# Own float32 tiles for the first six feature tiles' weights in a fused Mamba-2 and SwiGLU kernel, with a new order of steps

## The chip, the cores and the metric

The kernel runs on one NeuronCore of a Trainium2 chip. The metric is the device time of one execution in microseconds, lower is better. The engines named below are PE (TensorE matmuls; PEld its weight loads), DVE (VectorE), ACT (ScalarE), POOL (GpSimd) and SP (the queue from which nearly all DMAs are issued). Each engine works through its own queue in program order, and waits for the others by semaphores.

## What is computed

Two stages with a reshape between them. The first is a chunked state-space scan for 4 batches, 8 heads, 768 tokens, head dimension 32 and state dimension 16. The second is a SwiGLU feed-forward of 3072 tokens, width 256 and 1536 features.

```python
# stage 1, per chunk of tokens (x, a, B, C)
cum = np.cumsum(np.log(a_chunk), axis=-1)
L = np.exp(cum[..., :, None] - cum[..., None, :]) * causal
y = ((Cc @ Bc.T) * L) @ xc + (Cc @ state) * np.exp(cum)
state = np.exp(sum_la) * state + (Bc * np.exp(cum_last - cum)).T @ xc
# stage 2, x = y as (3072, 256)
xn = x / np.sqrt(mean(x * x) + 1e-6) * rms_g
out = (silu(xn @ w_gate) * (xn @ w_val)) @ w_out
```

The three weight matrices of stage 2 are double precision in memory, so they arrive as pairs of 32-bit words, and the kernel makes float32 values of them on the chip.

## The kernel before, in words

The 3072 tokens are six blocks of 512, and the 1536 features twelve tiles of 128 (`f` from 0 to 11), in six pairs (`j`). The program is a list of 1451 short steps, written out as one string, `order`; a loop at the end calls the function behind each step, and this order is the order of every engine's queue. A step is `block:name.numbers`, with `/slot` for one of three double banks of PSUM. The string was written for this program as a whole, so nothing reorders it later.

**Decoding weights.** There are 20 pieces: 0 to 3 are gate and value columns 0 to 127 and 128 to 255, 4 to 13 are the five further 256-column groups (even numbers gate, odd ones value), 14 to 19 are `w_out`. For each piece, `fetch` loads the words by a DMA on SP, `pow` (three ACT instructions) makes the exponents, `man` (two DVE instructions) the mantissas, and `wt` (one DVE instruction) their product. For gate and value columns below 768, `keep` then copies the float32 result by a DMA on SP into the big tile `wgv`, which is declared as fp32r. In the kernel before, `wt` writes columns 0 to 255 into the tile `wearly`, and columns 256 to 767 over the mantissa tile `m`, of which there are two buffers. `wearly` has the tag `sw3`: it shares its memory with the split weights of pair 3.

**Feature tiles 0 to 5 of block 0** are full float32 products (lines 868 and 878) that read `wgv` after the `keep`: `early.f.s` for tiles 0 and 1, on tokens not yet normalised (`norm.f` on DVE scales them afterwards), and `gate.f` for tiles 2 to 5. `silu.f` (ACT) and `hid.f` (DVE) finish each.

**All other feature products** use operands split in a leading and a trailing part. `sw.j.k` (three DVE instructions) splits a weight, and `kt.j.k` (a DMA) writes its leading part to `wgv`. `xm`, `xs`, `xh`, `xl` split the tokens. `D.f.k` (line 952) is the cross product, `W.f.k` (ACT, line 956) scales it, `G.f.k` (line 963) adds the main products, then come `silu` or `silug` and `hid` or `hidg`. They begin once `switch.0` and `switch.1` have given up the first two slots of PSUM, that is after `hid.5`.

**Stage 1** works on pairs of chunks: `bc` and `x` load B, C and x; `turn`, `T`, `Tt` transpose; `mask`, `sums`, `exp` make decays; `g`, `gg` the C-B products and `L`, `L1` their decay on DVE; `scale`, `A`, `S` the states; `y.p` the outputs. For later pairs decays make a round trip through DRAM: `row`, `rowe`, `rowout` store them, `dT` and `spread` load them, `Td` uses `dT`. At the start, `a` is loaded, turned (`aT`), clipped (`la0`) and its logarithm taken; from it come `c`/`cx`, `d`/`dx` and `r`/`parts`.

**From one block to the next**: after the last `y`, `sq`, `ms`, `rs` take the norm, `rb` spreads it by a round trip through DRAM, `xn` applies it, and the splits follow; meanwhile PE works on the output products `o` (block 0, line 975) or `O` (line 1033) of the running block.

**DMA semaphores.** SP and the four loads issued by ACT (half of `bc.0` and `bc.1`) share eight semaphores in turn. Each DMA instruction first waits until the DMA before it on its semaphore has landed, so at most eight are under way, and all that stands behind a waiting one on its queue waits too.

Of the kernel before, what the change touches and what calls it, by code (L numbers as in the profile page):

```python
# [21 lines left out]
def kernel(  # L22
# [33 lines left out]
    nc = tc.nc  # L56
# [79 lines left out]
    wg, wv = wgvf[:, 0], wgvf[:, 1]  # L136
    wearly = const.tile([P, 2, 2, 256], FP32, tag="sw3", name="wearly")
# [15 lines left out]
    def fetch(*ks):  # L153
        for k in ks:
            n, c, w = pieces[k]
            if n == "o":
                src, dst, shape = wsrc[n][:, c:c + w], wo[:, c:c + w], (w, DM)
            else:
                src = wsrc[n][:, :, 2 * c:2 * (c + w)]
                dst = wearly[:, "gv".index(n), :, c:c + w] if c < 256 else None  # L160
                shape = (2, w)
# [49 lines left out]
    def keep(k):  # L211
        n, c, w = pieces[k]
        src = wearly[:, "gv".index(n), :, c:c + w] if c < 256 else parts.pop((k, "w"))
        nc.sync.dma_start(out=wgv[:, "gv".index(n), :, c:c + w].bitcast(FP32), in_=src)
# [648 lines left out]
    def products_gv(f, gv):  # L863
        ps["gv", f] = gv
        fs = slice(f * P, (f + 1) * P)
        for k, w in enumerate((wg, wv)):
            for t in range(2):
                nc.tensor.matmul(out=gv[:, k], lhsT=w[:, t, fs], rhs=xns[0][:, t],  # L868
                                 start=(t == 0), stop=(t == 1))


    def products_early(f, s, gv):
        ps["gv", f] = gv
        fs = slice(f * P, (f + 1) * P)
        tk = slice(s * 256, s * 256 + 256)
        for k, w in enumerate((wg, wv)):
            for t in range(2):
                nc.tensor.matmul(out=gv[:, k, tk], lhsT=w[:, t, fs], rhs=yts[0][:, t, tk],
# [320 lines left out]
    def of_chunk(n, fn):  # L1199
# [40 lines left out]
        0:sq.1 0:pow.6 0:man.3 0:wt.2 0:pow.3 0:mask.3/1 0:early.0.0/0 0:keep.2 0:yt.1 0:bc.2  # L1240
        0:mask.2/2 0:parts.1 0:sums.3 0:man.6 0:wt.6 0:exp.3 0:wt.3 0:ms.0 0:fetch.13 0:early.0.1
        0:keep.6 0:keep.3 0:row.0 0:rowe.1 0:rowout.1 0:turn.2 0:sums.2 0:fetch.9 0:rs.0 0:T.2
        0:man.4 0:scale.2 0:early.1.0/1 0:wt.4 0:keep.4 0:norm.0 0:xn.0 0:exp.2 0:xm.0.0 0:ydone.1
        0:early.1.1 0:Tt.2.0 0:fetch.8 0:pow.7 0:xs.0.0 0:x.2 0:man.7 0:silu.0 0:rowe.0 0:fetch.10
        0:wt.7 0:gate.2/0 0:keep.7 0:pow.9 0:rowout.0 0:man.9 0:wt.9 0:sw.3.1 0:dT.2 0:hid.0
        0:Tt.2.1 0:norm.1 0:pow.8 0:bc.4 0:xm.0.1 0:man.8 0:wt.8 0:sw.3.0 0:gate.3/2 0:man.10
        0:silu.1 0:Td.2 0:xs.0.1 0:hid.1 0:pow.10 0:wt.10 0:gg.2/1 0:silu.2 0:L1.2.2 0:fetch.11
        0:kt.3.1 0:L1.2.3 0:xh.0.0 0:xh.0.1 0:hid.2 0:kt.3.0 0:A.2 0:pow.11 0:silu.3 0:pow.12
        0:scale.4 0:L.2.0 0:sw.4.0 0:man.11 0:fetch.14 0:wt.11 0:gate.4/1 0:hid.3 0:silu.4 0:man.12
        0:hid.4 0:x.3 0:S.2 0:bc.3 0:ydone.0 0:gate.5/0 0:silu.5 0:scale.3 0:y.2/2 0:xl.0.0 0:hid.5  # L1250
        0:yt.2 0:sq.2 0:ydone.2 0:switch.1 0:switch.0 0:D.6.0 0:dT.3 0:D.6.1 0:bc.5 0:W.6.0 0:D.7.0
# [151 lines left out]
```

## Time and profile before

| | us |
|---|---|
| three runs, median | 433.31 |
| three runs, lowest and highest | 427.08 and 433.46 |
| the profiled execution, as timed | 433.31 |
| its span, first to last instruction | 431.6 |

The execution's time is 1.7 us above its span. Some points in that span, from the timeline of each engine:

| point | us from the start |
|---|---|
| `la0`, the clipped logarithm's input | 4.4 to 4.8 |
| `d`, first products from the logarithms | 12.2 to 13.5 |
| `y.0` begins on PE | 32.7 |
| `gate.2` begins | 53.1 |
| second half of `gg.2` begins | 69.0 |
| `gate.5` ends | 82.5 |
| `hid.5` ends; first `D` of block 0 | 83.9; 84.2 |
| `y.3` ends | 94.2 |
| `o.11` ends | 134.5 |
| first `D` of blocks 1 to 5 | 123.1, 188.0, 253.8, 314.5, 372.6 |

"PEclk" in the views is the share of full clock that was granted to TensorE. Where it is 0.50, a matmul takes about twice as long. The busy time of PE is modelled from pipelined instructions and can hide that.

### The profile page before, as it was taken

To read this page: it belongs to the slowest core of one execution; us is meant where nothing else is said; L and a number is where in the kernel's file an instruction comes from. 1 tells how busy PE (TensorE), PEld (TensorE's weight loads), DVE (VectorE), ACT (ScalarE), POOL (GpSimd) and SP (SyncE) were. 2 spreads that over 40 slices of the span, in tenths; PEclk is the share of its full clock that TensorE was granted. 3 is DMA by queue.
4 is the path that set the end of the run, shared out by engine and by line. 5 is a ranking of instruction groups with operands and counts; after the bars stand their busy time and mean duration, and the time that the engine had idled before them with its cause. 6 is when DMAs were issued, how large, how long until landed. Compare 5 with 4: busy or idle time off the path is not lost.

```text
span 431.6 us, 9229 instructions
## 1 busy us (share of the span) xinstructions
PE 400.3 (93%) x3749; PEld 318.5 (74%) x3749; DVE 255.9 (59%) x545; ACT 256.9 (60%) x450; POOL 38.4 (9%) x57
## 2 busy tenths in 40 slices
PE   6797964999899999899979999998999989999997
PEld 3465722578688788897758997877987869978897
DVE  5555869799899547864355863446823434713551
ACT  1766787297998648265548644666674536366310
POOL 2201000010032001120011210100130001000000
PEclk9657895899999999999999999999999999999999
DMA  8725869659427228300154100203000001100001
GB/s 146 191 55 137 245 128 205 108 167 222 123 80 121 50 49 148 57 14 0 27 125 87 31 24 10 79 2 115 2 26 0 2 2 31 51 24 2 0 2 49
DMA packets 98034, 31.69 MB, mean 73 GB/s; under 512 B 77608, under 2 KB 91816, under 8 KB 97992
## 3 DMA queue, kind: packets, MB, share of 16 engines
q1 hardware_dynamic: 93832, 30.85, 30.6%
q10 hardware_dynamic: 4160, 0.26, 0.7%
q8 instruction: 29, 0.48, 0.5%
q14 instruction: 13, 0.11, 0.1%
HBM read 22.64 MB, written 3.74 MB: 61 GB/s over the span
## 4 chain that ended last, share of the span: by engine, by line
PE 72%; DVE 10%; ACT 7%; DMA 3%; issue 3%; SPq 3%; ACTq 0%; DVEq 0%
PE gv L963 24%; PE o L1033 18%; PE gv L952 13%; PE o L975 3%; PE y L711 3%; PE gate L868 2%; SPq L122 1%; PE g L567 1%; PE g L574 1%; DVE m L200 1%; DMA wr<-in_moe_w_val_dram 1%; DVE S L663 1%; DMA roots<-r 1%; DVE L L479 1%; DMA cr<-in_C_dram 1%
## 5 line engine op out<-in xcount | busy, mean ns | idle before, releaser
L963 PE MATMUL gv<-xh,wgv 128*128 128x512 f32 x264 | 109.1, 413 | 3.4 <-DMA wgv<-top 2.0
L963 PE MATMUL gv<-xl,mw 128*128 128x512 f32 x264 | 104.5, 396 | 0.0
L956 ACT ACTIVATE gv<-gv 128x512 f32<-128x512 f32 x132 | 73.7, 587 | 40.6 <-PE gv L952 40.0
L971 DVE SCALAR_TENSOR_TENSOR h<-gv,u 128x512 f32<-128x512 f32 x66 | 45.2, 689 | 81.3 <-PE gv L963 72.4
L952 PE MATMUL gv<-xs,sw 128*128 128x512 f32 x264 | 79.0, 411 | 2.8 <-DVE h L971 2.5
L968 ACT ACTIVATE u<-gv 128x512 f32<-128x512 f32 x66 | 39.5, 603 | 45.8 <-PE gv L963 43.9
L963 PEld LDWEIGHTS gv<-xh,wgv 128*128 128x128 f32 x264 | 50.1, 190 | 20.0 <-ACT gv L956 9.4
L952 PEld LDWEIGHTS gv<-xs,sw 128*128 128x128 f32 x264 | 45.9, 189 | 15.5 <-DVE h L971 4.0
L963 PEld LDWEIGHTS gv<-xl,mw 128*128 128x128 f32 x264 | 50.2, 190 | 9.4 <-DVE xl L848 0.2
L487 POOL TENSOR_SCALAR_AFFINE_SELECT L<-L 64x512 f32<-64x512 f32 x32 | 24.4, 762 | 115.3 <-ACT L L485 113.8
L1033 PE MATMUL o<-two,s 128*128 128x128 f32 x240 | 32.7, 277 | 1.3 <-DVE s L999 0.8
L1033 PE MATMUL o<-wo,h 128*128 128x128 f32 x240 | 33.8, 275 | 0.0
L1033 PEld LDWEIGHTS o<-two,s 128*128 128x128 f32 x240 | 30.1, 191 | 3.1 <-DVE s L999 1.2
L1033 PEld LDWEIGHTS o<-wo,h 128*128 128x128 f32 x240 | 31.2, 191 | 1.6 <-ACT u L968 0.4
L1033 PE MATMUL o<-two,h 128*128 128x128 f32 x240 | 30.8, 276 | 0.1
L1033 PEld LDWEIGHTS o<-two,h 128*128 128x128 f32 x240 | 28.8, 192 | 0.6 <-DVE h L1003 0.2
L1049 ACT COPY v<-o 128x256 f32<-128x256 f32 x15 | 5.6, 372 | 37.0 <-PE o L1033 37.0
L761 POOL TENSOR_TENSOR sq<-sq,sq 128x512 f32<-128x512 f32 (+1 forms) x6 | 7.4, 1236 | 169.9 <-issue 88.1
L975 PE MATMUL o<-wo,h 128*128 128x256 f32 x96 | 22.2, 379 | 0.0
L975 PEld LDWEIGHTS o<-wo,h 128*128 128x128 f32 x96 | 18.2, 189 | 2.8
L1006 DVE TENSOR_TENSOR s<-s,h 128x256 f32<-128x256 f32 x30 | 14.7, 518 | 8.9 <-PE o L1033 8.9
L1060 DVE TENSOR_TENSOR ob<-v,o 128x256 f32<-128x256 f32 x18 | 7.3, 416 | 18.5 <-PE o L1033 17.5
(183 smaller groups left out, 567.2 us busy)
## 6 DMA issues: line engine op xcount, KB each, us to landing
L<-rowd SPq DMA_DIRECT2D x32, 128.0 KB, 3.8
xr<-in_x_dram SPq DMA_DIRECT2D x24, 128.0 KB, 4.3
wgv<-top SPq DMA_DIRECT2D x12, 256.0 KB, 4.1
wr<-in_moe_w_out_dram SPq DMA_DIRECT2D x6, 512.0 KB
wr<-in_moe_w_val_dram SPq DMA_DIRECT2D x5, 512.0 KB
wr<-in_moe_w_gate_dram SPq DMA_DIRECT2D x5, 512.0 KB, 5.8
out_dram<-ob SPq DMA_DIRECT2D x9, 256.0 KB, 2.2
br<-in_B_dram SPq DMA_DIRECT2D x22, 64.0 KB, 3.4
```

The costliest lines, as they stand in the source:

```text
L487: nc.gpsimd.affine_select(out=L[r], in_=L[r], pattern=[[0, NH], [1, HC]], compare_op=ALU.is_ge, fill=0.0, base=0, channel_multiplier=-1)
L711: nc.tensor.matmul(out=y[2 * k + u][rows, (2 * n + i) * HC:(2 * n + i + 1) * HC], start=(k, u, rows.start) not in opened, stop=True, skip_ ...
L761: nc.gpsimd.tensor_tensor(out=sqs[blk][:, tk], in0=sqs[blk][:, tk], in1=sq2, op=ALU.add)
L868: nc.tensor.matmul(out=gv[:, k], lhsT=w[:, t, fs], rhs=xns[0][:, t], start=(t == 0), stop=(t == 1))
L952: nc.tensor.matmul(out=g, lhsT=Sw[f // 2][:, k, t, (f % 2) * P:(f % 2 + 1) * P], rhs=xs[blk][:, t], start=(t == 0), stop=True, skip_group_ ...
L956: nc.scalar.activation(out=GV[f, k], in_=GV[f, k], func=AF.Copy, scale=-BETA * BETA / (BETA + 1.0))
L963: nc.tensor.matmul(out=GV[f, k], lhsT=lhsT, rhs=rhs, start=False, stop=True, skip_group_check=True)
L968: nc.scalar.activation(out=us[f], in_=GV.pop((f, 0)), func=AF.Silu, scale=ONE)
L971: nc.vector.scalar_tensor_tensor(out=hidden_of(blk, f), in0=GV.pop((f, 1)), scalar=ONE, in1=us.pop(f), op0=ALU.mult, op1=ALU.mult)
L975: nc.tensor.matmul(out=o, lhsT=hs_[blk, f // 2][:, f % 2, k // 2, (k % 2) * P:(k % 2 + 1) * P], rhs=wo[:, f], start=opens, stop=(f == NF - ...
L1006: nc.vector.tensor_tensor(out=Sh[j], in0=Sh[j], in1=tiles_of_h(blk, j)[0], op=ALU.subtract)
L1033: nc.tensor.matmul(out=o[t] if apart else o[:, t * P:(t + 1) * P], lhsT=lhsT[:, t], rhs=rhs, start=(k in (1, 2, 4, 5) and j == 0 and (apar ...
```

## The change

The float32 weights of columns 0 to 767 get three tiles of their own, `whole_w[0..2]`, of 256 columns each. They carry the tags `sw3`, `sw4` and `sw5`, and so share memory with the split weights of pairs 3, 4 and 5; before, only `wearly` did so, with pair 3. `wt` writes there, the float32 products read there, and `keep` copies from there to `wgv`.

```diff
-    wg, wv = wgvf[:, 0], wgvf[:, 1]
-    wearly = const.tile([P, 2, 2, 256], FP32, tag="sw3", name="wearly")
+    whole_w = [const.tile([P, 2, 2, 256], FP32, tag="sw%d" % (j + NF // 4), name="whole_w")
+               for j in range(NF // 4)]
+
+    def whole(n, c, w):
+        return whole_w[c // 256][:, "gv".index(n), :, c % 256:c % 256 + w]
...
-                dst = wearly[:, "gv".index(n), :, c:c + w] if c < 256 else None
+                dst = whole(n, c, w) if c < DF // 2 else None
...
     def keep(k):
         n, c, w = pieces[k]
-        src = wearly[:, "gv".index(n), :, c:c + w] if c < 256 else parts.pop((k, "w"))
-        nc.sync.dma_start(out=wgv[:, "gv".index(n), :, c:c + w].bitcast(FP32), in_=src)
+        nc.sync.dma_start(out=wgvf[:, "gv".index(n), :, c:c + w], in_=whole(n, c, w))
...
-        for k, w in enumerate((wg, wv)):
+        for k, n in enumerate("gv"):
             for t in range(2):
-                nc.tensor.matmul(out=gv[:, k], lhsT=w[:, t, fs], rhs=xns[0][:, t],
+                nc.tensor.matmul(out=gv[:, k], lhsT=whole(n, f * P, P)[:, t], rhs=xns[0][:, t],
                                  start=(t == 0), stop=(t == 1))
...
-                nc.tensor.matmul(out=gv[:, k, tk], lhsT=w[:, t, fs], rhs=yts[0][:, t, tk],
+                nc.tensor.matmul(out=gv[:, k, tk], lhsT=whole(n, f * P, P)[:, t], rhs=yts[0][:, t, tk],
```

All lines of `order` are new: it holds the same 1451 steps in another order (slots apart). The stretch up to the end of `y.3` in both:

```diff
-        0:warm 0:zeros 0:a 0:never 0:idle.7 0:ones 0:ident 0:after 0:whole16 0:kinks 2:exps
-        0:ident16 0:hmask 0:fetch.5 0:whole 0:mask.0.0/0 0:eps 0:upto 0:mid 0:upto2 0:bc.0 0:tmask
-        0:fetch.0 0:aT 0:la0 0:x.1 0:mask.1.1/2 0:log 0:log4.0.4 0:head 0:mask.0.1/1 0:log4.4.2
-        0:c*2 0:after2 0:mids 0:r.0 0:d 0:bc.1 0:turn.0.1 0:part 0:x.0 0:cx 0:part2 0:man.5 0:sel
...
-        0:sq.1 0:pow.6 0:man.3 0:wt.2 0:pow.3 0:mask.3/1 0:early.0.0/0 0:keep.2 0:yt.1 0:bc.2
-        0:mask.2/2 0:parts.1 0:sums.3 0:man.6 0:wt.6 0:exp.3 0:wt.3 0:ms.0 0:fetch.13 0:early.0.1
-        0:keep.6 0:keep.3 0:row.0 0:rowe.1 0:rowout.1 0:turn.2 0:sums.2 0:fetch.9 0:rs.0 0:T.2
-        0:man.4 0:scale.2 0:early.1.0/1 0:wt.4 0:keep.4 0:norm.0 0:xn.0 0:exp.2 0:xm.0.0 0:ydone.1
-        0:early.1.1 0:Tt.2.0 0:fetch.8 0:pow.7 0:xs.0.0 0:x.2 0:man.7 0:silu.0 0:rowe.0 0:fetch.10
-        0:wt.7 0:gate.2/0 0:keep.7 0:pow.9 0:rowout.0 0:man.9 0:wt.9 0:sw.3.1 0:dT.2 0:hid.0
-        0:Tt.2.1 0:norm.1 0:pow.8 0:bc.4 0:xm.0.1 0:man.8 0:wt.8 0:sw.3.0 0:gate.3/2 0:man.10
-        0:silu.1 0:Td.2 0:xs.0.1 0:hid.1 0:pow.10 0:wt.10 0:gg.2/1 0:silu.2 0:L1.2.2 0:fetch.11
...
+        0:warm 0:a 0:set 0:bc.0 0:ident 0:bc.1 0:ones 0:x.0 0:zeros 0:mean 0:head 0:upto 0:x.1
+        0:never 0:after 0:mid 0:fetch.0 0:upto2 0:mids 0:ident16 0:idle.7 0:fetch.1 0:whole16
+        0:mask.0.0/0 0:whole 0:hmask 0:tmask 0:part 0:gcol 0:part2 0:sel 0:mask.1.1/2 0:after2 0:aT
+        0:kinks 0:la0 0:mask.0.1/1 0:log4.0.4 0:fetch.5 0:r.0 0:eps 0:parts.0 0:log 0:d 0:log4.4.2
+        0:dx 0:c*2 0:cx 0:scale.0 0:log4.6.2 0:turn.0.1 0:bc.2 0:T.0.1 0:Tt.0.0.1 0:sums.0.1
...
+        0:r.1 0:y.0/1 0:yt.0 0:keep.5 0:sq.0 0:y.1/2 0:rowe.0 0:fetch.4 0:pow.6 0:dT.2 0:wt.1
+        0:keep.1 0:parts.1 0:mask.3/1 0:sums.3 0:sq.1 0:early.0.0/0 0:man.2 0:yt.1 0:pow.2 0:scale.2
+        0:rowout.0 0:pow.9 0:man.6 0:wt.6 0:ms.0 0:wt.2 0:keep.2 0:early.0.1 0:man.3 0:man.9 0:exp.3
+        0:wt.9 0:rs.0 0:norm.0 0:pow.3 0:wt.3 0:fetch.8 0:bc.3 0:turn.2 0:xn.0 0:xm.0.0 0:pow.4
+        0:man.4 0:mask.2/2 0:sums.2 0:exp.2 0:wt.4 0:keep.3 0:early.1.0/1 0:early.1.1 0:xs.0.0
+        0:norm.1 0:x.2 0:fetch.10 0:T.2 0:Tt.2.0 0:silu.0 0:hid.0 0:pow.7 0:man.7 0:wt.7 0:Tt.2.1
+        0:xh.0.0 0:Td.2 0:gate.2/0 0:xm.0.1 0:gg.2/1 0:keep.7 0:silu.2 0:pow.8 0:gate.3/2 0:sw.3.1
+        0:hid.2 0:fetch.12 0:kt.3.1 0:man.8 0:wt.8 0:x.3 0:L1.2.2 0:keep.6 0:L1.2.3 0:L.2.0 0:A.2
+        0:gate.4/1 0:sw.3.0 0:xh.0.1 0:fetch.11 0:silu.1 0:hid.1 0:S.2 0:gate.5/0 0:keep.4 0:silu.3
+        0:fetch.13 0:scale.3 0:y.2/2 3:table 0:xs.0.1 0:pow.10 0:man.10 0:wt.10 0:silu.4 0:man.11
+        0:pow.11 0:hid.3 0:silu.5 0:pow.12 0:sq.2 0:ydone.2 0:kt.3.0 0:hid.4 0:xl.0.0 0:xl.0.1
+        0:ydone.0 0:hid.5 0:ydone.1 0:switch.1 0:switch.0 0:D.7.0 0:D.6.0 0:W.6.0 0:sw.4.0 0:wt.11
+        0:sw.4.1 0:W.7.0 0:yt.2 0:x.4 0:man.12 0:wt.12 0:D.6.1 0:fetch.14 0:G.6.0 0:bc.5 0:turn.3
+        0:T.3 0:kt.4.0 0:D.7.1 0:Tt.3.0 0:tok 0:D.9.0 0:scale.5 0:silug.6 0:tokout 0:G.7.0 0:W.6.1
+        0:dT.3 0:kt.4.1 0:G.6.1 0:Tt.3.1 0:sw.5.0 0:bc.4 0:kt.5.0 0:Td.3 0:W.7.1 0:S.3 0:silug.7
+        0:x.5 0:W.9.0 0:D.8.0 0:hidg.6 0:G.7.1 0:pow.13 0:fetch.16 0:W.8.0 0:man.13 0:gg.3/2
+        0:L1.3.3 0:D.8.1 0:W.8.1 0:hidg.7 0:G.9.0 0:silug.9 0:pow.14 0:G.8.0 0:silug.8 0:D.10.0
+        0:L.3.0 0:W.10.0 0:L1.3.2 0:scale.4 0:G.8.1 0:y.3/2 0:wt.13 0:sw.5.1 0:fetch.15 0:D.11.0
...
```

Instruction counts in the two programs: PE, DVE, POOL and SP have the same instructions (by kind and shape); ACT has 31 loads of its function tables in place of 36. The numbers of PE, DVE, ACT and DMA instructions per step are otherwise equal. The steps `exps`, `table` and `set` load a table by name; further loads are put in by the compiler where the next ACT function needs another table.

## Prediction

> **What bounds the kernel now.** I read the page's busy shares first, then the windows by stage, then the waits up to the first `D`, then the chain of waits, and last the timelines of single engines.
>
> ```profile
> PE 400.3 (93%) x3749; PEld 318.5 (74%) x3749; DVE 255.9 (59%) x545; ACT 256.9 (60%) x450; POOL 38.4 (9%) x57
> ```
>
> PE is busy 93% of the span, but that is an average over stages. The windows (columns: us, PE, PEld, DVE, ACT, POOL busy, granted clock, DMA share, GB/s):
>
> ```profile
> 0.00:13.00 13.00, 7.45 (x33) 4.38 (x33) 6.29 (x30) 3.30 (x7) 2.94 (x13) 1.00 0.90 147
> 13.00:36.90 23.90, 23.01 (x204) 13.71 (x207) 15.14 (x37) 14.68 (x28) 2.21 (x5) 0.50 0.47 145
> 36.90:64.20 27.30, 21.22 (x167) 12.81 (x158) 18.89 (x37) 23.13 (x34) 1.46 (x2) 0.94 0.66 157
> 64.20:77.80 13.60, 6.75 (x50) 3.33 (x51) 13.12 (x25) 8.50 (x13) 0.00 (x0) 0.50 0.95 183
> 77.80:84.20 6.40, 6.40 (x140) 3.32 (x138) 4.20 (x11) 1.19 (x2) 0.00 (x0) 1.00 0.68 137
> 84.20:134.00 49.80, 47.71 (x383) 38.07 (x382) 46.61 (x92) 44.46 (x79) 6.23 (x6) 1.00 0.57 142
> 164.30:431.60 267.30, 257.50 (x2356) 219.26 (x2354) 134.43 (x283) 141.84 (x250) 21.30 (x27) 0.99 0.15 35
> ```
>
> The late phase is PE's. Between 64.2 and 77.8 the bound is DVE (13.12 of 13.60), with PE half idle at half clock. Between 84.2 and 134 DVE (46.61 of 49.80) and PE (47.71) are both nearly full. The waits up to 84.2 (us in total, times, longest) name the holes:
>
> ```profile
> ACT early L415 <- DMA cr<-in_C_dram: 6.1, 1, 6.1
> PE g L574 <- DVE T L548: 5.1, 1, 5.1
> PE d_ps L391 <- ACT early L415: 4.4, 1, 4.4
> PE g L574 <- DVE h L892: 3.3, 1, 3.3
> ```
>
> The first and third are one hole: ACT must issue half of `bc.1` before it may run `cx`, its issue waits for an earlier load on the same semaphore, and PE's `d` waits for `cx`. The second is `Td.2`. The chain of waits (start, us, what) shows this start, and table loads of ACT in the middle:
>
> ```profile
> 8.03 3.10 DMA cr<-in_C_dram
> 11.16 0.46 ACTq L122
> 11.66 0.53 ACT early L415
> 12.23 0.94 PE d_ps L391 x4
> ...
> 38.41 1.28 ACT L1225
> ...
> 53.19 1.28 ACT L899
> ...
> 55.12 1.28 ACT L1121
> ```
>
> PE's timeline gives the price of half clock: the same sixteen float32 products, `gate.2` and `gate.3`, then `gate.4` and `gate.5`:
>
> ```profile
> 53.05 7.03 PE L868 MATMUL gate<-xn,wgv 128*128 128x512 f32 x16
> 72.97 9.54 PE L868 MATMUL gate<-xn,wgv 128*128 128x512 f32 x16 [1.06 <-DVE L L613]
> ```
>
> **The tiles.** Reading `whole_w` instead of `wgv` removes the wait of each float32 product for the `keep` DMA. It is worth 0: `keep.4` landed at 52.75, `gate.2` began at 53.05 behind PE's own `early.1.1`; `keep.7` landed at 62.2, `gate.4` began at 72.97, released by DVE. If a cover went, a `keep` (issue to landing some 4 us) would be its price. The `keep` stays, for the split products. Added: `sw.4` and `sw.5` now wait until `keep.4` to `keep.7` and `gate.2` to `gate.5` have read the shared memory. Behind a waiting `sw.4.0` on DVE stand `wt.11`, `sw.4.1` and the rest of pair 3; but the order puts `sw.4.0` behind `switch.0`, where `gate.5` and the keeps are past. Direct cost 0; indirect, below.
>
> **The start.** In after, `bc.0` and `bc.1` are issued first and wait only for the load of `a`; ACT need not stall behind `x.1`. Ahead of `la0` DVE has 4.1 us of rows, so `la0` at 6.0 to 6.4 against 4.4, and `d` at about 7.8 against 12.23: −4.4. But steps that lay in the hole now follow: `c*2` (1.25 us, pieces) and `row.0` (1.15, `r_ps` rows) fall into the stretch from `d` to `y.0`, 20.45 us long, where PE is busy 23.01 of 23.90. −4.4 + 2.4 = −2 at `y.0`; bounds −4.4 and 0. Weights come later: eight B and C loads go ahead of `fetch.0`, but `wt.0` is needed by `early.0.0` alone, at 45 us. On SP `fetch.4` moves behind `rowe.0`, which waits for ACT's table and `e_sb` (about 37 us, before 15.9); a weight load of its kind lands 5.8 us after issue (page, part 6), so at 43, and `man.4`, which needs it, ran at 45.3: cost 0, and 2 to 3 us of DVE's wait if `rowe.0` comes late.
>
> **From `y.0` (32.7) to the first `D` (84.2), 51.5 us.** Three terms:
> - *Tables.* Before has four loads here (38.41, 53.19, 55.12, 61.89), after two (at `silu.0`, and `3:table`): 2 × 1.28 = −2.6, since three of the four are on the chain.
> - *`Td.2`.* From the end of `xn.0` (50.62) to `Td.2` (68.50), DVE has 14.4 us of rows. In after `sw.3.1` (1.81), `man.8` (1.11), `wt.8` (0.69), `sw.3.0` (1.81) and `man.10` (1.11), 6.5 us, stand behind it, and some smaller steps: 7.2 us remain. The 5.1 us wait goes. SP issues `dT.2` earlier too.
> - *Clock.* Without that hole `gate.4` and `gate.5` may run at full clock: 9.54 − 7.03 = −2.5.
>
> Sum −10.2. What is late next is DVE itself: its rows from `y.0` to `hid.5` sum to 40.4 before and 37.9 after, at a busy/sum ratio near 0.95. So after cannot be shorter than 37.9 × 0.95 + some 3 us until DVE's first step, 39; that allows −12.5. ACT's rows are 31 and 34, no bound. A new order has waits of its own that no row shows; before lost 51.5 − 39 = 12 to such waits. I take −8 of the 10.2 (bounds −12 and −3): first `D` at about 84.2 − 2 − 8 = 74.
>
> **What the shared memory pushes behind the first `D`.** Before had `sw.4.0` at 72.8, in the lead; in after `sw.4.0`, `sw.4.1`, `sw.5.0` follow `hid.5`. DVE's rows from there to `scale.4`, the last input of `y.3`, sum to 14.9 us after; before, the same stretch (to `L1.3.2`) 9.75, and took 8.1. PE's own rows to the end of `y.3` are 13.1 against 8.6. To the end of `o.11`: DVE 55.8 against 50.4, PE 47.8 against 46.7, taken 49.7. To `1:D.11.1`, PE is the larger: 83.4 against 75.3 (taken 80.1), DVE 76.2 against 67.6. PE's sum over the whole rest is the same in both, 321.3 us (taken 347.4), so the DVE-bound stretch costs only what PE idles: between 14.9 − 13.1 = 1.8 and 55.8 × 0.95 − 47.8 = 5.2. I take +3; bounds 0 and +5.2.
>
> **The late phase.** At each block's end PE lives on products that don't need the next block's norm. Their rows between the last `y` and the next first `D` sum to 27.4, 27.4, 32.4, 38.0 and 16.5 us before (the norm's way took 28.9, 28.5, 37.3, 39.3, 16.6), after to 19.4, 25.1, 38.2, 33.4, 26.1. The shortest cover, 19.4, is above the shortest way that before shows, 16.6. So 0, bounds −4 and +4: the whole late loss of PE is 267.3 − 257.5 = 9.8, and a new order could win or lose some 40% of that. Five table loads fewer in all (36 to 31), three of them before the first `D`; the two late ones, 2.6 us of ACT, cost nothing where PE is the bound.
>
> **Sum.** −2 − 8 + 3 + 0 = −7. The profiled execution ran 433.31 with a span of 431.6, and is itself the median: 433.3 − 7 = 426.3. Bounds of the terms, not all at one end: 419 to 432.
>
> **A rule of the skill.** The trace first: the clock fell at 12.99, after PE idled 4.4 us, and stayed at 0.50 to 36.9 although PE was busy 23.01 of 23.90. The Trainium skill, "TensorE: Matmul & The Clock Gate", Part 1, says otherwise of such a stretch: one window of about 3.4 us with sustained activity releases the throttle, one idle window brings it back. By that rule the clock should have returned by about 20, and a lead without the 4.4 us hole would run at full clock: the sum would be some 10 us lower, by my estimate from this page. The rows say that this lead's small products, spaced by waits on DVE and ACT, do not count as sustained, so I leave the half clock of the lead in the main sum.
>
> **The rivals.**
> 1. *The lead runs at full clock.* Without the hole at 7.8 to 12.2 the gate may never close. For it: full clock from 6.16 to 12.99 with PE busy 7.45 of 13.00. Against: the shares above. From `d` to `y.0` the chain's PE pieces sum to 16 us; at full clock half of that, 8, and one more from the `y` pieces (2.55): 426 − 9 = 417.
> 2. *The gain is hidden.* DVE's rows to `1:D.11.1` are 8.6 us more after; if block 1's first half is held by them, all of the 10 comes back: 433.
> 3. *Slower.* After the switch DVE is the bound and PE idles in pieces, so that the clock halves. It decides where PE idles over about 2 us of a 3.41 us window: between 40.30 and 43.71 PE was busy 1.36, and the next window ran at 0.50. Price: DVE stretch 55.8 and further waits, 8 us where I put 3, and five windows at half clock, 1.7 to 3.4 us each, 8 to 17: −10 + 8 + 13 = +11, 442 to 446. For it: 46.61 of 49.80 already. Against: full clock through that whole window in before.
>
> That the change doesn't do what it says is so in part: the DMA wait that the tiles remove was not one. Whatever comes, comes from the order.
>
> **How the numbers follow.** Main case 0.45, rival 1 0.15, rival 2 0.20, rival 3 0.20. A measurement of this kernel can tell about 2% (its three runs spread by 1.5%): under 424.6, over 442.0. Faster: two fifths of the main case (0.18), rival 1 (0.15) and a little of rival 2: 0.36. Slower: nearly all of rival 3 and a little late loss: 0.20. Same: 0.44. Range 417 to 442: it leaves out half of rival 1 and most of rival 3.
>
> **What would show it.** In the profile after: `d` near 7.8 and no wait of `cx` on a C load; `y.0` near 31; the wait of `g` L574 on `T` L548 gone; two table loads between `y.0` and the first `D`; first `D` near 74; `y.3` 12 to 15 us behind it (before 10); `o.11` 52 to 53 behind it (before 50.3); `wgv` no longer among the products' releasers at L868. The main case's own range is 419 to 432. I am wrong if the first `D` is past 80, if PEclk is 0.50 behind it, or if first `D`s of blocks 2 to 5 drift from each other by more than 4 us against before.

## The result, and the profile after

| | before | after |
|---|---|---|
| median (lowest to highest) of the first comparison, us | 433.38 (427.08 to 438.85) | 407.62 (406.40 to 408.99) |
| profiled execution, us; its span | 433.31; 431.6 | 407.84; 406.1 |
| `d` begins | 12.23 | 6.18 |
| `y.0` begins | 32.68 | 21.91 |
| first `D` of block 0 | 84.18 | 61.73 |
| `o.11` ends | 134.45 | 114.50 |

The ratio of the times is 0.9452, with a 95% interval of 0.9346 to 0.9558; the medians differ by 25.8 us, where 7 were forecast. The ratios, here and below, leave out runs more than 1.5% above the fastest of their kernel, so they differ a little from the quotients of the medians. By stage of the two spans: up to `y.0` −10.8, from there to the first `D` −11.7, from there to the end of `o.11` +2.5, from there on −5.5.

The busy shares of the page, after, with its row of granted clocks (40 equal slices of the span):

```profile
PE 387.1 (95%) x3749; PEld 309.1 (76%) x3749; DVE 252.7 (62%) x545; ACT 248.8 (61%) x445; POOL 36.2 (9%) x57
PEclk9989999999999999999999999999999999999999
```

PE is busy 13 us less with as many products, at a higher clock: in the trace before, 44.4 us of the span are at 0.50, after 3.4. The windows of the four stages (columns as in the prediction), first after, then two of the same stages before:

```profile
0.00:21.90 21.90, 19.08 (x165) 11.22 (x165) 16.75 (x59) 13.83 (x29) 5.08 (x17) 0.98 1.04 166
21.90:61.70 39.80, 33.44 (x419) 19.38 (x418) 36.55 (x74) 31.12 (x50) 1.46 (x2) 0.97 0.81 210
61.70:114.50 52.80, 49.62 (x387) 38.81 (x388) 49.69 (x99) 40.02 (x77) 1.60 (x2) 1.00 0.62 157
114.50:406.10 291.60, 284.98 (x2781) 239.73 (x2779) 149.68 (x315) 163.84 (x292) 28.09 (x36) 1.00 0.17 39
```

```profile
32.70:84.20 51.50, 38.57 (x424) 22.77 (x423) 38.50 (x78) 33.43 (x50) 1.46 (x2) 0.79 0.74 169
134.50:431.60 297.10, 287.30 (x2784) 242.47 (x2782) 151.24 (x316) 161.15 (x290) 25.57 (x32) 0.99 0.17 39
```

In the middle DVE was busy 38.50 us of 51.50 before and 36.55 of 39.80 after. Its idle time fell from 13.0 to 3.25 us (−9.75), and 1.95 us of its work went elsewhere: together the −11.7. In the late stage, from the end of `o.11` on, PE's idle time fell from 9.8 to 6.6.

PE's timeline after, at the places shown of before:

```profile
45.18 0.65 PE L577 MATMUL g<-T 32*64 32x128 f32 x20 [0.23 <-DVE T L551]
45.77 3.70 PE L870 MATMUL gate<-xn,whole_w 128*128 128x512 f32 x8
51.02 7.13 PE L870 MATMUL gate<-xn,whole_w 128*128 128x512 f32 x16 [0.25 <-DVE L L616]
```

The wait for `Td.2` is 0.23 us where it was 5.07, and `gate.4` with `gate.5` takes 7.13 where it took 9.54.

### The profile page after: what moved, and what is told of

Read it like the earlier page. It is cut to its first block, busy times and chain, and to the rows that moved or that the text cites. A ratio compares the mean times of both kernels' runs of the same rounds, so it can differ in the third digit from the quotient of the medians.

```text
span 406.1 us, 9238 instructions
## 1 busy us (share of the span) xinstructions
PE 387.1 (95%) x3749; PEld 309.1 (76%) x3749; DVE 252.7 (62%) x545; ACT 248.8 (61%) x445; POOL 36.2 (9%) x57
## 4 chain that ended last, share of the span: by engine, by line
PE 66%; DVE 12%; ACT 9%; DMA 7%; issue 3%; SPq 1%; DVEq 0%; ACTq 0%
PE gv L964 25%; PE o L1034 19%; PE gv L953 13%; PE y L714 3%; DMA wgv<-top 2%; DMA roots<-r 2%; DMA r<-roots 1%; DMA wr<-in_moe_w_out_dram 1%; ACT e L191 1%; ACT e L192 1%; PE g L577 1%; DVE h L972 1%; DVE sw L938 1%; ACT gv L957 1%; DMA wr<-in_moe_w_gate_dram 1%
## 5 line engine op out<-in xcount | busy, mean ns | idle before, releaser
L964 PE MATMUL gv<-xh,wgv 128*128 128x512 f32 x264 | 107.6, 408 | 2.2 <-ACT gv L957 2.1
L972 DVE SCALAR_TENSOR_TENSOR h<-gv,u 128x512 f32<-128x512 f32 x66 | 45.4, 690 | 98.9 <-PE gv L964 79.4
L953 PE MATMUL gv<-xs,sw 128*128 128x512 f32 x264 | 80.8, 413 | 3.2 <-DVE h L972 1.6
L953 PEld LDWEIGHTS gv<-xs,sw 128*128 128x128 f32 x264 | 44.8, 189 | 17.7 <-ACT u L969 5.9
L490 POOL TENSOR_SCALAR_AFFINE_SELECT L<-L 64x512 f32<-64x512 f32 x32 | 22.7, 711 | 128.1 <-ACT L L488 126.6
L1034 PEld LDWEIGHTS o<-wo,h 128*128 128x128 f32 x240 | 30.4, 192 | 1.5 <-ACT u L969 0.6
L976 PEld LDWEIGHTS o<-wo,h 128*128 128x128 f32 x96 | 18.1, 189 | 3.2 <-DVE wo L210 0.4
L191 ACT ACTIVATE e<-wr,kinks 128x512 int16<-128x512 int16 (+1 forms) x20 | 14.2, 709 | 6.2 <-DMA wgv<-top 2.8
L1007 DVE TENSOR_TENSOR s<-s,h 128x256 f32<-128x256 f32 x30 | 13.2, 452 | 7.1 <-PE o L1034 7.0
```

What stands on the lines that cost most here:

```text
L191: nc.scalar.activation(out=k16, in_=words16, func=AF.Relu, scale=1.0 / 16, bias=kinks[:, 0:1])
L490: nc.gpsimd.affine_select(out=L[r], in_=L[r], pattern=[[0, NH], [1, HC]], compare_op=ALU.is_ge, fill=0.0, base=0, channel_multiplier=-1)
L953: nc.tensor.matmul(out=g, lhsT=Sw[f // 2][:, k, t, (f % 2) * P:(f % 2 + 1) * P], rhs=xs[blk][:, t], start=(t == 0), stop=True, skip_group_ ...
L964: nc.tensor.matmul(out=GV[f, k], lhsT=lhsT, rhs=rhs, start=False, stop=True, skip_group_check=True)
L972: nc.vector.scalar_tensor_tensor(out=hidden_of(blk, f), in0=GV.pop((f, 1)), scalar=ONE, in1=us.pop(f), op0=ALU.mult, op1=ALU.mult)
L976: nc.tensor.matmul(out=o, lhsT=hs_[blk, f // 2][:, f % 2, k // 2, (k % 2) * P:(k % 2 + 1) * P], rhs=wo[:, f], start=opens, stop=(f == NF - ...
```

## The experiments

"Order of before" and "changed order" are the two strings. Splicing means: the steps of one string up to a named step, then all that remain in the order of the other. `*n` behind a step puts n products whose results are not used ahead of its own. Every group of runs had runs of the kernel before beside it; their medians were 433.35 (x1 to x4), 433.47 (x5 to x8), 430.99 (x9 to x12), 433.02 (x13 to x16) and 432.9 (x17, x18). Points inside a kernel come from its one profiled execution. Among profiled executions with the changed start, `d` alone began anywhere from 6.0 to 7.1 us, so differences of one microsecond in single points mean little. The changed kernel itself was timed in the first comparison alone; x12_r1fill and x18_notable, which hardly differ from it, came to 407.26 and 407.05 later.

**x1_tiles: the tiles alone.** The changed kernel with the order of before.

> The own tiles with every step in the order of the kernel before. If no product had waited for a keep (the prediction's reading), the time stays within 1% of before, 429 to 437 us, and the first D of block 0 at 83 to 85 us. If the tiles themselves took waits away, the first D comes before 80 us and the time is 428 us or less. If the shared memory costs something by itself (sw.4.0 behind gate.3, sw.5.0 behind gate.5), the first D comes after 86 us.

Measured: 433.9, ratio 0.9935 (0.9889 to 0.9982); first `D` at 78.8. The tiles move the time by at most 1%; nearly all of the result is the order. The early first `D` does not speak for the tiles: the profiled execution was, at 428.37, one of the two quickest of ten, and its lead ran at half clock to 27.57 us, that of before to 36.88, with the same order. `gate.2` began behind `early.1.1` in both. That two executions of one order can differ that much fits the spread of the kernel before, 11.8 us in its first four runs, against 2.6 of the changed one.

**x2_fill: the idle stretch before `d` filled.**

```diff
-        ... 0:mask.0.1/1 0:log4.4.2 0:c*2 0:after2 0:mids 0:r.0 0:d 0:bc.1
+        ... 0:log4.4.2 0:c*2 0:after2 0:mids 0:r.0 0:mask.0.1*40/1 0:d 0:bc.1
```

> The kernel before with 40 extra bf16 matmuls of 256 columns on PE between r.0 and d, in the 4.4 us in which PE idled; nothing else is sooner. Theory A (that idle stretch closed the clock gate, and the closed gate is most of the slow lead): d still starts at 12 to 13 us, the granted clock is 1.00 to at least 20 us, y.0 begins at 27 to 29 instead of 32.7, and the time falls by 3 to 6 us. Theory B (the lead's small products lose the clock whatever stands before them, as the prediction's main case had it): clock 0.50 from 17 us at the latest, y.0 at 32 to 33, time within 1 us of before.

Measured: 433.21, ratio 1.0009 (0.9936 to 1.0081). `y.0` began at 29.99, between the two forecasts. The windows of x2_fill:

```profile
10.15:13.57 3.42, 3.42 (x29) 2.62 (x27) 0.00 (x0) 1.88 (x3) 1.27 (x2) 1.00 1.09 140
13.57:16.98 3.41, 1.76 (x34) 0.84 (x32) 2.65 (x8) 3.37 (x5) 1.61 (x4) 1.00 0.82 257
16.98:20.40 3.42, 2.89 (x12) 1.74 (x12) 2.60 (x9) 3.05 (x8) 0.00 (x0) 0.50 0.59 187
```

The filling held the clock to 16.98, and then the next gap lost it: PE was busy 1.76 of 3.41 while ACT (3.37 of 3.41) worked through the end of `pow.5`, `dx`, the table load `set` and `exp.0.1`. The half clock then lasted 10.2 us, where before has 23.9. So that one hole does not decide by itself whether the lead loses its clock; theory A falls in that form.

**x3_bcfirst: `bc.0` and `bc.1` first.**

```diff
-        0:warm 0:zeros 0:a 0:never ... 0:bc.0 ... 0:bc.1 ...
+        0:warm 0:zeros 0:a 0:bc.0 0:bc.1 0:never ...
```

> The kernel before with bc.0 and bc.1 issued directly behind the load of a, nothing else moved. ACT no longer stalls, d starts at 7 to 9 us in both theories. Theory A: the clock stays at 1.00 past 20 us, y.0 at 22 to 25, first D at 74 to 77, time 423 to 426 us. Theory B: clock 0.50 by 17 us, y.0 at 28 to 29, first D at 80, time about 429 us.

Measured: 430.5, ratio 0.9936 (0.9873 to 0.9999). `d` at 7.53, as the prediction had it for the changed kernel, but clock 0.50 from 12.28 and `y.0` at 28.64. A new hole had taken the place of the old one, 2.85 us behind `d`: DVE waited 3.4 us for the load of weight piece 5 with `parts.0` queued behind it, and ACT had `pow.5` in front of `dx`.

**x4_start: the changed start alone**, spliced behind `y.1`.

> The changed kernel's steps up to y.1, then all others in the order of the kernel before (own tiles). y.0 at 21.5 to 22.5 us as in the changed kernel. If the start's gain is a thing by itself, the rest follows 10.8 us earlier: first D at 73 to 74, time 421 to 424 us. If the middle stage of before is held by something that doesn't move with y.0 (weight loads, decoding on ACT), the first D comes after 77 us and the time is 427 us or more.

Measured: 431.45, ratio 0.9972 (0.9931 to 1.0014). `y.0` at 21.87, 10.8 us sooner, and full clock to 32.18; but `early.0.1` at 41.15 where before had 45.30, and the first `D` at 79.4. The waits of x4_start between 26 and 42 us:

```profile
PE e L441 <- DVE yt L773: 8.6, 1, 8.6
DVE whole_w L210 <- ACT e L194: 6.6, 1, 6.6
ACT e L191 <- DMA wr<-in_moe_w_gate_dram: 3.0, 1, 3.0
```

Read from the last: ACT waits in `pow.4` for the load `fetch.4`, which SP had issued at 24.84 behind a `keep`. `pow.2`, a table load and `sq.1` stand behind it on ACT. DVE waits for `pow.2` and then for `sq.1` before it can run `yt.1`, and PE waits 8.6 us for that. The early start is not passed on by this middle, whose loads and decoding have not moved.

**x5_mid: the changed order up to `switch.0`**, then before's.

> The changed kernel's steps up to switch.0, then the order of the kernel before (own tiles). First D of block 0 at 61.5 to 62.5 us. If the lead-in up to the switch makes nearly all of the gain, the rest takes what it takes in before, 347 us: span 409, time 409 to 413. If the late order of the changed kernel matters for itself (its rest took 344.4) or the rest of before is held by weight loads that don't move, the time is 415 us or more.

Measured: 422.11, ratio 0.9751 (0.9669 to 0.9834). First `D` at 61.58, but the rest took 358.5 us where it took 347.4 in before and 344.4 in the changed kernel. Four windows of x5_mid:

```profile
61.60:65.19 3.59, 1.65 (x6) 1.03 (x6) 3.49 (x7) 3.53 (x8) 1.19 (x1) 1.00 0.81 95
65.19:68.60 3.41, 3.13 (x10) 2.58 (x10) 3.27 (x9) 2.49 (x8) 0.00 (x0) 0.50 1.02 243
160.76:164.17 3.41, 0.97 (x9) 0.78 (x7) 1.88 (x3) 2.16 (x4) 1.74 (x2) 1.00 0.90 111
164.17:171.00 6.83, 6.06 (x28) 6.06 (x29) 4.29 (x11) 0.00 (x0) 0.45 (x1) 0.50 0.01 1
```

This is rival 3's mechanism, in a splice instead of the changed kernel: DVE and ACT full behind the switch, PE short of work, half clock after it; and again at 160.76, where PE was busy 0.97 of 3.41. Behind the changed lead the changed late order is worth 14 us; behind the lead of before it was not tried.

**x6_startb: before's start, changed order from `y.1` on.**

> The kernel before up to y.1, then the changed kernel's order (own tiles). y.0 at 30 to 33 us. If the middle's gain is a thing by itself, 39.8 us lie between y.0 and the first D as in the changed kernel: first D at 70 to 73, time 414 to 419. If the middle can be quick only behind the early start, the first D comes after 76 us and the time is 421 or more. If weights that before's start has decoded already shorten it, the first D comes before 69.

Measured: 421.84, ratio 0.9744 (0.9657 to 0.9831). `y.0` at 33.29, first `D` at 73.81: 40.5 us between them, as many as in the changed kernel (39.8). The middle's gain needs neither the early start nor its clock, though the time stayed above the 414 to 419 that went with it. From here to the changed kernel only the start differs, and that is worth 14.2 us (407.62), where x4_start gained 1.9 by it, within the noise.

**x7_pow4: x4_start with `pow.4` moved** from before `sq.1` to before `man.4`.

> The kernel of x4_start with one step moved: pow.4, which made ACT wait for the load fetch.4 (landed at 29.95), goes from before sq.1 to just before man.4. Theory (ACT's queue order, not the tiles and not the clock, held the middle of x4_start): PE's 8.6 us wait ahead of sums.3 is gone, early.0.1 starts at 33 to 36 instead of 41.15, first D at 72 to 75, time 423 to 427. Rival (weights are late altogether, the next load or the table load takes its place): early.0.1 at 39 or later, time 429 or more.

Measured: 427.75, ratio 0.9867 (0.9759 to 0.9974). `early.0.1` at 37.95 and the time lie between the two forecasts; the first `D`, at 78.7, hardly moved from x4_start's 79.4, with a `y.0` 2 us later (23.85): 54.8 us from `y.0` to the first `D`, where x4_start has 57.6. `pow.4` was one of several things that held the middle. The rest of the span took 3.5 us less as well (348.3 for 351.8), without the half clock that x4_start has from 175.54 to 182.36, so the 3.7 us between the medians are not the middle's alone.

**x8_td: `Td.2` alone moved** behind `xm.0.1`, in the kernel before.

> The kernel before with Td.2 alone moved forward, behind xm.0.1 and so ahead of man.8, wt.8, sw.3.0 and man.10 (4.7 us of DVE). The prediction's term: PE's 5.1 us wait shrinks to 1 or less, gate.4 begins at 68 to 69 instead of 73 and its clock comes back sooner: first D at 78 to 80, time 426 to 429. Rival (Td.2 then waits for the landing of dT.2, or gate.4 waits for L.2.0 on DVE as before): gate.4 at 71 or later, time 431 or more.

Measured: 433.55, ratio 1.0072 (1.0019 to 1.0124). `Td.2` ran at 64.25 instead of 68.50, and `gate.4` began at 73.56: it waits for `L.2.0`, which kept its place on DVE (72.8). Two waits of PE in x8_td, from 60 to 85 us:

```profile
PE A_ps L639 <- DVE L L619: 5.9, 1, 5.9
PE g L574 <- DVE T L548: 0.2, 1, 0.2
```

The wait for `Td.2` is gone, and PE waits 5.9 us for the next step that it needs from DVE (`L1`, line 619; 1.0 in before). The 5.1 us wait was real and worth nothing.

**x9_piece5: the start of before without piece 5 in front**, then the changed order.

```diff
-        0:warm 0:zeros 0:a ... 0:bc.0 ... 0:bc.1 ... 0:man.5 ... 0:pow.5 ... 0:wt.5 ... 0:set ... 0:keep.5 ...
+        0:warm 0:zeros 0:a 0:bc.0 0:bc.1 ... 0:r.1 0:man.5 0:pow.5 0:wt.5 0:keep.5 0:fetch.6 ...
```

> The kernel of x6_startb (start of before, then the changed order) with three edits in the start: bc.0 and bc.1 directly behind the load of a, the second load of the same ACT table (set) left out, and the decoding of weight piece 5 (man.5, pow.5, wt.5, keep.5), which stood ahead of parts.0 on DVE and of dx on ACT and waited there for its weight load until 9.26 us, moved behind r.1. Theory C (the first products' operands stood behind weight decoding and a table load in the queues of DVE and ACT; PE so starved loses its clock): PE has no hole over 1 us from d to y.0, clock 1.00 to at least 18 us, y.0 at 21.5 to 24 us as in the changed kernel (x3_bcfirst, which kept piece 5 in front: 28.6), first D 40 us later, time 409 to 413. Rival (the clock falls in this lead whatever comes first, because its products are issued in another order): 0.50 before 17 us, y.0 at 26 or later, time 415 or more.

Measured: 421.68, ratio 0.9805 (0.9749 to 0.9861). `d` at 7.85, no gap over 1.1 us, and still the clock fell at 12.92. The windows of x9_piece5:

```profile
9.51:12.92 3.41, 2.08 (x36) 1.15 (x36) 3.17 (x12) 1.54 (x4) 1.57 (x3) 1.00 1.17 141
12.92:16.33 3.41, 3.29 (x20) 1.75 (x24) 2.81 (x7) 2.94 (x8) 0.00 (x0) 0.50 0.95 284
```

`y.0` came at 27.23, 6 us sooner than in x6_startb, and the first `D` at the same time (74.4): SP stood still from 31.3 to 36.2 behind `bc.2`, and ACT waited for a weight load to 41.6. The rival's three numbers came true, not theory C's. The gaps that theory C named were gone, so they alone do not explain the lost clock of this start; PE was still busy only 2.08 of 3.41 in the window before it fell.

**x10_tables: two table loads more** in the changed kernel (`2:exps` behind `0:silu.0`).

> The changed kernel with one more load of the exp table put directly behind silu.0, so that silu.2 needs another load of its own: two loads of 1.28 us more between y.0 and the first D, as many there as before. The prediction's term: 2.6 us, so the first D at 64 to 64.5 and the time 409.5 to 411. Rival (ACT has slack there, DVE is the bound of that stage): first D within 0.7 us of 61.7, time within 1 us of the changed kernel.

Measured: 409.13, ratio 0.9515 (0.9457 to 0.9574). First `D` at 64.66, 2.9 us later, of which `y.0` already accounts for 1.7; `gate.3` was stretched by a half clock from 47.5 to 54.4. The time is 1.5 us up, with intervals that overlap the changed kernel's.

**x11_pow4in: `pow.4` put where before has it**, ahead of `sq.1`, in the changed kernel.

> The changed kernel with one step put where the kernel before has it: pow.4 ahead of sq.1 on ACT, where it waits for the load fetch.4 (issued at 26.9, landed 4 us later). Theory (one decode step ahead of its weights in ACT's queue holds the whole middle): sq.1 ends at 33 to 35 instead of 29.7, early.0.1 at 35 to 38 instead of 30.9, first D at 65 to 68, time 411 to 415. Rival (DVE is the bound of the middle and hides it): first D at most 2 us later, time at most 410.

Measured: 412.0, ratio 0.958 (0.9521 to 0.9638). Two waits of x11_pow4in, from 22 to 50 us:

```profile
DVE yt L773 <- ACT sq L755: 5.6, 1, 5.6
ACT e L191 <- DMA wr<-in_moe_w_gate_dram: 2.6, 1, 2.6
```

`sq.1`, with its part on POOL, ended at 35.98 (29.73 in the changed kernel), `early.0.1` began at 37.90, and the first `D` came at 67.94, 6.2 us later, of which `y.0` already accounts for 1.8. At the end one step moved by 27 places of the order costs 4.4 us. That includes its clock: 0.50 from 34.2 to 41.0.

**x12_r1fill: `0:r.1*5`** in the changed kernel.

> The changed kernel with five bf16 matmuls of 256 columns ahead of r.1, in the 0.6 us in which PE waits there (20.4 to 20.96), just before the one window at half clock that the changed kernel has (20.6 to 24.0). If that window is lost to this gap: clock 1.00 throughout, y.0 ends 1 us sooner, early.0.0 1 to 2 us sooner; time 406 to 407.6, since the chain behind runs on ACT and DVE. If the window is lost to the sum of gaps since 17 us: no change, 407 to 408.

Measured: 407.26, ratio 0.9476 (0.9428 to 0.9525); clock 0.50 from 21.07 to 24.49 as before. `r.1` with its filling began at 20.82, against 20.96 without: the filling uses `r.1`'s own bank and so came behind the gap, not into it. Inconclusive.

**x13_exps: one table load of 1.28 us ahead of `exp.0.1`** in the changed kernel (`2:exps`), where before has `set`.

> The changed kernel with one more load of the ACT table that is already loaded, 1.28 us, put ahead of exp.0.1, where the kernel before has such a load (set). If PE's lead holds the clock only by being dense (theory C), the gap of 1.3 us behind it makes a window of 3.41 us with PE busy 0.5 to 0.6, the clock falls to 0.50 near 13 to 16 us and stays there until y.0, which begins at 26 to 28 instead of 21.9; the clock alone is then worth 3 to 5 us. If the changed lead holds its clock by the kind of its products, the load costs its own time: y.0 at 23.0 to 23.5.

Measured: 411.97, ratio 0.9591 (0.9448 to 0.9733). The windows of x13_exps:

```profile
8.18:11.60 3.42, 3.42 (x44) 2.11 (x42) 3.29 (x12) 2.70 (x4) 1.90 (x4) 1.00 1.38 187
11.60:15.01 3.41, 2.42 (x30) 1.47 (x28) 0.91 (x3) 3.41 (x9) 0.81 (x2) 1.00 1.01 237
15.01:18.42 3.41, 3.31 (x15) 2.45 (x15) 3.21 (x6) 2.15 (x6) 0.00 (x0) 0.50 0.78 120
25.25:28.66 3.41, 3.41 (x38) 1.89 (x35) 2.83 (x3) 0.37 (x1) 0.00 (x0) 0.50 0.03 11
```

One window with PE at 2.42 of 3.41, and the lead runs at half clock from 15.01 to 28.66, four windows, though PE is all but fully busy in them. `exp.0.1` came 1.45 us later, `y.0` 4.9 us later (26.79); the 3.4 us between the two came with the half clock. The first `D` was 5.1 us later and the time 4.4 us up. In this middle a late start is passed on nearly in full.

**x14_group: `Td.2` to `L.2.0` as a group** moved ahead of the weight decoding, in the kernel before.

```diff
+        0:norm.1 0:gate.3/2 0:Td.2 0:gg.2/1 0:L1.2.2 0:L1.2.3 0:A.2 0:L.2.0 0:pow.8 0:bc.4 0:xm.0.1 0:man.8 0:wt.8 ...
```

> The kernel before with Td.2, gg.2, L1.2.2, L1.2.3, A.2 and L.2.0 moved as one group behind norm.1 (gate.3 ahead of them on PE), so that man.8, wt.8, sw.3.0, man.10, wt.10 and hid.1, hid.2 stand behind on DVE. Theory D (gate.4 waits for the slot of PSUM that L.2.0 gives up, and L.2.0 stood behind 7 us of other DVE work): gate.4 begins at 67 to 69 instead of 73, first D at 78 to 80, time 426 to 429. Rival (the landing of dT.2, issued at 59.3 behind rowe.0, is as late as the DVE work was): gate.4 at 70 or later, first D past 81, time 430 or more.

Measured: 434.17, ratio 1.0106 (1.0002 to 1.0211). `gate.4` at 66.36, 6.6 us sooner; first `D` at 83.33, 0.9 sooner. DVE's timeline in x14_group:

```profile
63.64 0.42 DVE L548 TENSOR_TENSOR T<-tp,dT 128x256 f32<-128x256 f32 x1
65.62 0.68 DVE L613 TENSOR_TENSOR L<-g,L 128x512 f32<-128x512 f32 x1
...
80.03 0.42 DVE L653 TENSOR_TENSOR A<-A_ps,tmask 128x128 f32<-128x128 f32 x2
80.36 0.92 DVE L663 SCALAR_TENSOR_TENSOR S<-S,fcol,A 128x64 f32<-128x64 f32 x3
```

`Td.2` (L548) and `L.2.0` (L613) came forward by 4.9 and 6.6 us, and `S.2` (L663), which `y.2` needs, by 0.3: in before it ran at 80.67. DVE is busy 16.41 of the 17.00 us from 66 to 83. What stood in front of the group now stands behind it, and `S.2` behind all of it.

**x15_early: x14_group with `rowe.0` and `dT.2` early as well**, behind `sums.2`.

> As x14_group, and rowe.0 and dT.2 moved ahead of silu.0, directly behind sums.2 (in before, rowe.0 follows silu.0, costs a table load of its own and is issued at 56.7). Theory D with its rival settled: Td.2 waits for no DMA; gate.4 at 63 to 66, no half clock behind gate.3, first D at 73 to 76, time 422 to 425. If DVE's weight work is the bound by itself in that stretch, the first D stays past 78 and the time at 427 or more.

Measured: 435.66, ratio 1.0151 (1.0023 to 1.0279). `gate.4` at 63.67, first `D` at 80.2, 4 us sooner than before; by block 2's `D.0.0` all of it was given back (197.3 against 196.7), with the clock at 0.50 in two further windows on the way. Its rival came true: the first `D` stays past 78 and the time past 427, as it should where DVE's work is the bound by itself.

**x16_all: all named causes together**, behind the changed start.

> The changed kernel's steps up to y.1, then the order of before with the edits of x7_pow4 and x15_early. If the named causes add up (start, pow.4 in front of sq.1, the group from rowe.0 to L.2.0), the first D comes at 66 to 70 us and the time is 414 to 419, most of the way to the changed kernel's 407.6. If something unnamed holds before's middle, the first D stays past 72 and the time past 421.

Measured: 426.54, ratio 0.9907 (0.9853 to 0.9961); first `D` at 73.2 in a profiled execution that was, at 430.83, the longest of ten. From `y.0` to the first `D` 51.3 us, where x4_start has 57.6 and the changed kernel 39.8: in this execution the named steps are 6 us of 18. By the medians they are 4.9 us of the 23.8 from x4_start to the changed kernel. What holds the rest was not found; no step that was moved by itself accounts for it.

**x17_head: 2.2 us of DVE work more** in the changed kernel (`head` six times behind `xn.0`).

> The changed kernel with the reduction head (0.37 us on DVE) repeated six times behind xn.0: 2.2 us more for DVE, nothing else. If DVE bounds the middle from there on (busy 36.55 of its 39.80 us), the first D comes 1.8 to 2.5 us later, 63.5 to 64.2, and the time is 409 to 410. If ACT's decoding is the bound and DVE has slack behind xn.0, the first D is at most 0.8 us later and the time at most 408.3.

Measured: 409.53, ratio 0.9449 (0.9395 to 0.9504), whose interval overlaps the changed kernel's; the median is 1.9 us above. First `D` at 63.43, 1.7 later, with `y.0` in its place (21.98): more work on DVE comes out at the end of the middle nearly in full, as it should where DVE is the bound. It need not be the only one: in x6_startb the same stretch took 40.5 us with DVE busy for only 34.77.

**x18_notable: without `3:table`.**

> The changed kernel without the step 3:table, a load of the silu table at 50.4 us while that table has been in place since 39.96 (silu.0) and nothing between asks for another. ACT gains 1.28 us in the middle. From x10, where 2.56 us more of ACT put the first D 2.9 us and the time 1.5 us later, half as much the other way: first D at 60.3 to 61.2, time 406.4 to 407.2. If DVE alone bounds the middle: no change, 407.3 to 407.9.

Measured: 407.05 (406.16 to 407.96), ratio 0.9398 (0.9359 to 0.9436). First `D` at 61.65, 0.08 us sooner: nothing in that stage, and 0.6 us in the median is within its spread. ACT's load was covered. No version measurably beats the changed kernel.

The changed order on the old tiles was not tried; whether it needs the new ones stays open.

## Why the prediction was wrong

The direction was right, the size was not: 426.3 forecast, 407.6 measured, below the range's end of 417. Step by step:

1. **The tiles, 0.** Right (x1_tiles, within about 1%).
2. **The start, −2: wrong, −10.8.** Two steps failed. The first is the time of `la0`: the forecast put it at 6.0 to 6.4, behind 4.1 us of DVE's rows, but these began at 0.88 and were done by 4.4, and DVE then waited for PE's `aT`:

```profile
4.88 0.36 DVE L324 TENSOR_SCALAR early<-aT 128x192 f32<-128x192 f32 x1 [0.48 <-PE aT L320]
```

From there to `d` it took 1.30 us, about what the forecast had, so `d` came at 6.18, not 7.8. The second is the step "I leave the half clock of the lead in the main sum". It was false, and so the stretch from `d` to `y.0`, which I had charged with 2.4 us more, took 15.7 us, not 20.45. I read the half clock as a property of the lead's small products. But the changed kernel has the same products, and every profiled kernel with the changed start held full clock to 20.8 us or later, except x13_exps, in which one table load more left PE short of work; all nine with before's start or a variant of it lost it between 9.8 and 17.0. So the order of the lead decides, and x13_exps shows that 1.3 us of ACT's time in it can lose the clock. Rival 1 was right that the lead can run at full clock. Its reason, the one hole ahead of `d`, was not enough: with the hole filled (x2_fill), removed so that another took its place (x3_bcfirst), or removed together with the next gaps (x9_piece5), the clock still fell. Which property of before's start loses it stays open.
3. **The middle, −8: right in kind, −11.7.** The bound of 39 us that the prediction took from DVE's sum was within 1 us of the truth (39.8). What failed is the reserve of 4.5 us (43.5 taken, 39 bound) for "waits of its own that no row shows": DVE idles 3.25 us in all, about the 3 us that the bound already had. Of the three terms below it, *clock* (−2.5) was right: 7.13 for 9.54. *`Td.2`* (−5.1) was not a term at all: x8_td and x14_group removed the wait and got nothing, because DVE owed the same work to the next steps that PE needs (`L1` and `L.2.0` in the one, `S.2` in the other). *Tables* (−2.6) are not settled as a term: x10_tables cost 1.5 us and x18_notable gained none that shows. The three summed to −10.2, near the truth, by chance: what changed was DVE's idle time, 13.0 less 3.25, and its work, less 1.95. One cause that the prediction did not see costs the changed kernel 4.4 us when it is put back (x11_pow4in): a decode step in ACT's queue ahead of its weights.
4. **Behind the first `D`, +3: the number right, in part by luck** (+2.5 up to `o.11`). The forecast counted what PE idles, 1.8 to 5.2. PE idles only 1.1 us more there (3.18 against 2.09); the other 1.4 are work of PE that before does behind `o.11`.
5. **The late phase, 0 with ±4: −5.5, outside.** The covers were sufficient: from the last `y` to the next first `D` it took 19.7, 26.3, 37.8, 34.3 and 26.7 us, each near the sum of its cover, and no wait of PE on the norm shows behind `o.11`. The forecast had less ground for it than it said, since it set the shortest cover against the shortest way, which belong to different blocks. What failed is the idle time of PE that the sum left as it was, 9.8: it fell by 3.2. Another 1.4 us of work (49.62 against 48.21) had moved ahead of `o.11`, and before loses a little to a window at half clock (224.62 to 228.03) that the changed kernel does not have. Which steps closed the gaps was not tried. One of the forecast's signs of being wrong shows here too: the first `D`s of blocks 2 to 5 come 18.5, 22.3, 24.1 and 25.2 us sooner, a drift of 6.6 where it allowed 4.
6. **The rivals.** Rival 2 (gain given back by block 1) did not happen: later shifts are passed on nearly in full in the changed order (x13_exps, 5.1 at the first `D`, 4.4 at the end). Rival 3 (slower) did not happen here, but its mechanism is what x5_mid shows in before's late order. The limit that it took from one window, 2 us of idle PE, does not hold: the changed kernel lost its clock behind a window with 0.7 us idle.
7. **The skill's rule.** Within each trace the changes of the clock lie multiples of 3.41 us apart. It fell behind windows with PE busy 2.08 and 2.42 of 3.41 and no gap over 1.1 us, and three full windows of before did not release it:

```profile
23.23:26.64 3.41, 3.41 (x36) 1.69 (x36) 1.64 (x4) 2.14 (x6) 0.00 (x0) 0.50 0.00 0
26.64:30.06 3.42, 3.42 (x22) 2.33 (x18) 2.92 (x7) 2.65 (x4) 0.00 (x0) 0.50 0.11 30
30.06:33.47 3.41, 3.41 (x26) 1.92 (x26) 1.79 (x3) 0.46 (x1) 0.00 (x0) 0.50 0.85 262
```

The Trainium skill, "TensorE: Matmul & The Clock Gate", Part 1, gives a window of about 3.4 us for both directions. The multiples agree with that. The page speaks of an idle window for the fall and of one busy window for the release; these rows agree with neither, and the measurement decides. The forecast that the prediction worked out from the page, full clock without the hole, came true in the changed kernel, but not in x9_piece5, which has no such hole either.

## What to carry to other kernels

In a stage that one engine bounds, sum that engine's work and its idle time, and forecast the idle time; a wait on another engine's timeline was worth nothing here where the bounding engine owed the same work to the next consumer (x8_td, x14_group). In each engine's queue, look for a step that waits on a transfer ahead of steps that don't: one such step cost 4.4 us (x11_pow4in). A speed-up early in a program can be lost if the loads and decoding behind it don't move too: the same new start gave 1.9 us, within the noise, ahead of one later order (x4_start) and 14.2 ahead of the other (x6_startb to the changed kernel).

## What the runs showed of the hardware that was not expected

The clock's two directions are not alike in this lead. One window of 3.41 us with PE busy 2.08 (x9_piece5) or 2.42 (x13_exps) lost it, while the changed kernel kept it through one with 2.52 in `y.1`'s time, after it had lost it to one with 2.71:

```profile
17.73:21.14 3.41, 2.71 (x19) 1.68 (x20) 3.23 (x10) 3.34 (x6) 0.00 (x0) 1.00 0.92 285
21.14:24.56 3.42, 3.42 (x50) 2.20 (x49) 2.72 (x4) 1.11 (x3) 0.00 (x0) 0.50 0.99 318
24.56:27.97 3.41, 2.52 (x86) 1.59 (x78) 3.27 (x9) 2.39 (x5) 0.73 (x1) 1.00 0.53 174
```

So neither the busy share of a window nor its longest gap tells by itself what will happen. Lost before 17 us, it mostly stayed lost for three to eight windows, many of them with PE fully busy; lost at 21.14 in the changed kernel or at 43.71 in before, it came back after one. Why busy windows of the lead don't release it was not isolated. The windows are not tied to the program's start (full clock is first recorded at 3.7 to 10.6 us). With the same order, the lead ran at half clock for five windows in x1_tiles and for seven in before, and the spans are 426.7 and 431.6; that the place of the windows makes this difference is a reading, not tested.
